# A new hand-out order for 2,900 operations, with one-element activations ahead of five table loads

## The chip, the cores and the metric

The kernel runs on one NeuronCore of a Trainium2 chip. Five engines each follow a queue of their own: TensorE (PE, matrix products), VectorE (DVE), ScalarE (ACT), GpSimd (POOL) and SyncE (SP), which issues all transfers of this kernel. Queues meet only through semaphores, and within a queue the order is fixed when the program is built. The metric is device time in microseconds; less is better. Three runs of the kernel before gave 535.62, 537.95 and 539.45 us, median 537.95.

## The reference

Two independent layers of width 576 over 2,048 positions, put side by side in the output. All data are float32.

```python
def _A_ref(u, log_A_real, A_imag, C_real, C_imag, log_dt, D_skip):
    dt = jnp.exp(log_dt)
    A = -jnp.exp(log_A_real) + 1j * A_imag
    C = (C_real + 1j * C_imag) * dt[:, None]
    P = jnp.exp((A * dt[:, None])[:, :, None] * pos[None, None, :])
    K = 2.0 * jnp.einsum("dn,dnl->dl", C, P).real
    y = irfft(rfft(u_t, 2L) * rfft(K, 2L))[:, :, :L]
    return y.transpose(0, 2, 1) + u * D_skip

def _B_ref(x, wqkv, w_phi, wo):            # 32 heads of 18
    q, k, v = split(x @ wqkv)
    pq, pk = q @ w_phi[h], k @ w_phi[h]
    phi = concat(softmax(p), softmax(-p))  # for q and for k
    kv, z = phi_k^T v, sum_s phi_k
    o = (phi_q kv) / (phi_q z + 1e-6)
    return o.reshape(B, S, D) @ wo
...
return jnp.concatenate([a, b], axis=-1)
```

Layer A is a long convolution: a kernel K of 2,048 taps for each of 576 channels is made from 128 complex modes and applied through a Fourier transform. Layer B is linear attention with a learned softmax feature map.

## The kernel before

**Layer B.** `fold` multiplies the feature map into the key and query weights (five blocks of heads; five products of up to 126 columns each, L448 by way of `mm`), and splits the result and the value and output weights (`whole`) into a high part `wh` and a remainder `wl`, so that a float32 product becomes three products of a faster type. `key_tile` takes one of 16 tiles of 128 positions: it loads x (`zo`), splits it (`x`, L542 and L463), multiplies it in three products of 378, 378 and 396 columns, makes the softmax features `e` and adds into one accumulator (`ps<-e,v`: 32 small products, one a head). `query_tile` does the same for queries, divides, and multiplies by the output weights. The first key product needs the first three folded blocks only; the second needs all five and a third of the value weights.

**Layer A.** `u_first` transforms the input (`ps<-kb,w`), in 16 steps. 18 pairs of channel groups (called group 0 to 17 here) make the convolution kernel: `phases` adds up integer phases on POOL into `cs` (a copy from `pi`, L899, and five doubling steps, L903; `cs` has two buffers, so a new pair waits until PE has read the old one), `waves` turns them into sines on ACT (L913, L920, L921), `group` multiplies them by exponentials on DVE (`cs`, `E`) and contracts them on PE (`ps<-E,cs`: 32 products for each half). `k_first`, `product` and `last` are the Fourier steps; they pass data through DRAM.

**What sets the order.** Each of these functions only records operations (`Plan.op`): an engine, or two of which either may do it, a function, and what it depends on. `Plan.run` then hands out all 2,900 in the sequence of the table `ORDER`. An entry `1143+2/2/8` is operation 1143, with 2 filler matmuls of zeros ahead of it (L227, they write a tile that the operation overwrites), and buffer slots 2 and 8 for the tiles that it opens; a `*` takes the second of its two engines. So the table sets the order in each engine's queue, the engine of the flexible operations (mostly copies out of PSUM, ACT or DVE, and element-wise operations on SBUF tiles, POOL or DVE), and which buffer is used again when. Semaphore waits follow from it.

**Table loads.** ScalarE holds one set of functions at a time. When the program is built, an ACT_TABLE_LOAD is put in front of an activation that needs another set. A wait for one semaphore is part of the activation itself, behind the load; where an activation waits for two, one wait stands as an instruction of its own in front of the load.

Of the kernel before, what the change touches and what calls it, by code (L numbers as in the profile page):

```python
# [170 lines left out]
class Plan:  # L171
# [58 lines left out]
    def run(self, order):  # L230
# [3 lines left out]
        for x in order:  # L234
            x, *slots = x.split("/")
            x, _, fill = x.partition("+")
            second, k = x.endswith("*"), int(x.rstrip("*"))
# [8 lines left out]
            self.emit(o, o[5][0] if second else o[0], int(fill or 0))
# [36 lines left out]
1197/12 239/1 1332 1333 1177/15 397 1289/10 383 1515 51/12 1339/1 1387 1388 1473/0 1334 271/0 1288 482 384/13 1307/14
1237/11 1335 1522 52* 1340 213/0 53 1474 1523/16 385 1290/3/7/1/6/1 1475 1166 1336 272/2 1294 1291 1252 1256/0 347/10
1255 386 1476 1342 1293 44 1525 270/0 388*/1 387 1477 55/6 274/2 1292 1337 278 389 1295 56/3 132/4 45 1349/13 1478
57/4 58/3 59 1533 60/5 275 1352 276/2 390 277 1338 1518 1479 1199/8 381/1 1198 391/12 1519/1 62 1697 1520 61 63 73
1348 1341 64*/4 65 1524 1343 158/18 279 214* 240/6 273/7 215 218/5 74 398 133* 392/5 280*/6 1344 393/0 66 67/17 1345
1346 289 1296 241* 54/1 394 1482 1480 1350 1200/6/0/3/4/8 1526 1207/12 242 223/1 217/1 1203 68/3 1202 1204 290 281*
1481 395 399 69/4 245/2 224 225/9 70* 1201 1527 1389/0 1390 1432/1 1433 348/11 1205 219/3 1239/8 221 1483 1434 1696
75* 1435 1528 1529 220 222 235 1436 1437 1488/0/10/7 1530 483 484 485 1531 1698 236* 282 1501/4/1/12 1486/7 1503/6  # L290
251/2 1484/5 1489 49/1 401/13 1546/1 246/3 71 1487 1217/1 226*/5 250 216/2 1491 283/17 1492 1206 1485 1504 1532 76 400
1438 227 1297/16 243/3 1490 1545 284/6 134 228 285/0 252/5 1277/6 244/0 263 229/4 1534 1699 1703 1535/17 1208/5 262
1502 1493 1353 1494 137/5 230/3 1536 104/4 286* 1537 455/17 1439 1440 1238* 248 231/4 1499/3 428/11 1538 287 143/1
1508 1354 247 1539 1495/2/13/0 154 232 1540 378/4 136/7 349* 253/5 1509 350 1700 1500 1496 249 135/5 138/4 254 1317/10
1507 1704 1505 237 255 1506 1510/0 1541 233 142 140 155 144/8 139 1240/3/6/4/5/6 256/8 351/6 291* 402/7 1511 1497 238
141 1244 320/3 429/10 1542 1543 1243 1242* 1241 1246 292 1267/7 1445/5/3/1 352/4 159/12 145*/6 1355 1441 1442 430*
257/3 293/8 258/2 431 353/3 1544 1219/11 146 1218 355/5 1705/1 356 1547/0 432/7 1245 1548 1549 1443/7 354/6 1550 1498
1551 359 1552 1715 358 147 1444 370 361/4 357/4 1707 1447/2 435/4 371 1449 1446 1448 360 1512 1513 362 105/9 1553 160*
1452 434/6 1450 363 1209 148/12 1451 1210/7/3/0/2/2 1453 1356 321/6 1212* 161 1454/5 450/5 364/18 452 1214 259 440/0
1213 1220/4/2/3/0/11 451 149/1 403 260 1211 185/12 1216 1223 1222* 1221 150/6 1224 1225 1458/7/1/3 1460/3 1462/2 365/5  # L300
1215 163/4 1459 1461 1464 1463 264 433/0 1554 151 1455 1465 1226 1468 1227/11 1257/18 366/4 439 404 156 1556 1466 1467
152 167/3 265 1555 441/2 1469/7 162/8 367 157 1706 166 1557 1558/2/10/11 437 368 1357 496/13 164/3 168/5 405/9 1470
# [125 lines left out]
def body(tc, nc, i, out, ctx):  # L428
    pl = Plan()
# [15 lines left out]
    B, op = pl.buf, pl.op  # L445
# [39 lines left out]
    hp = B("hp", [128, 1])  # L485
# [669 lines left out]
```

## Time and profile before

| what | value |
|---|---|
| median of 3 runs | 537.95 us (535.62 to 539.45) |
| the profiled execution | 534.13 us, its span 532.4 us |
| granted clock of TensorE | 0.997 |
| PE, DVE, ACT, POOL busy | 510.1, 453.9, 410.4, 331.8 us |
| moved by DMA | 115.97 MB, mean 218 GB/s |
| table loads of ScalarE | 42 |
| filler matmuls | 94 |

An engine is busy here while at least one of its instructions runs. A row of the timeline gives the start, the length, the engine, the line, the operation with what it writes and reads, how many instructions were merged, and in brackets the idle time of the engine ahead of them with what ended it. "issue" in that place is time in which the engine waited for nothing that the profile shows. The rows of the groups give the busy time, the mean duration of one in ns, and the idle time ahead. Times are from the start of the span.

### The profile page before, as it was taken

To read this page: it belongs to the slowest core of one execution; us is meant where nothing else is said; L and a number is where in the kernel's file an instruction comes from. 1 tells how busy PE (TensorE), PEld (TensorE's weight loads), DVE (VectorE), ACT (ScalarE), POOL (GpSimd) and SP (SyncE) were. 2 spreads that over 40 slices of the span, in tenths; PEclk is the share of its full clock that TensorE was granted. 3 is DMA by queue.
4 is the path that set the end of the run, shared out by engine and by line. 5 is a ranking of instruction groups with operands and counts; after the bars stand their busy time and mean duration, and the time that the engine had idled before them with its cause. 6 is when DMAs were issued, how large, how long until landed. Compare 5 with 4: busy or idle time off the path is not lost.

```text
span 532.4 us, 20329 instructions
## 1 busy us (share of the span) xinstructions
PE 510.1 (96%) x8502; PEld 421.4 (79%) x8502; DVE 453.9 (85%) x988; ACT 410.4 (77%) x727; POOL 331.8 (62%) x379
## 2 busy tenths in 40 slices
PE   8899999999999888999999999999999999999996
PEld 6799898999988676788886777866688886667975
DVE  3899998999998878999998999889987769887572
ACT  4799989999879968989999879789876455555442
POOL 1568899977988875894586478858373435323210
PEclk9999999999999989999999999999999999999999
DMA  8888994623426486375578755797575787996687
GB/s 261 290 331 244 278 318 139 211 80 143 143 79 196 119 285 204 81 234 142 158 225 298 247 180 173 235 287 244 167 245 170 249 247 234 282 337 220 216 306 214
DMA packets 80512, 115.97 MB, mean 218 GB/s; under 512 B 12452, under 2 KB 57636, under 8 KB 80420
## 3 DMA queue, kind: packets, MB, share of 16 engines
q1 hardware_dynamic: 80420, 114.67, 67.4%
q8 instruction: 67, 1.10, 0.8%
q14 instruction: 25, 0.20, 0.1%
HBM read 65.63 MB, written 49.01 MB: 215 GB/s over the span
## 4 chain that ended last, share of the span: by engine, by line
PE 68%; DVE 9%; ACT 8%; POOL 7%; DMA 4%; issue 3%; SPq 1%; POOLq 0%; ACTq 0%; DVEq 0%
PE ps L448 65%; POOL cs L903 3%; PE ps L700 2%; DVE ac L467 1%; POOL e L463 1%; DVE cs L948 1%; ACT e L593 1%; DMA e<-in_wkT_dram 1%; DMA mg<-gd 1%; ACT cs L920 1%; DMA ff<-in_ff_dram 1%; POOL wl L531 1%; ACT cs L913 1%; ACT cs L921 1%; DMA zo<-in_xT_dram 1%
## 5 line engine op out<-in xcount | busy, mean ns | idle before, releaser
L448 PE MATMUL ps<-wh,x 128*128 128x288 f32 (+2 forms) x1008 | 241.0, 319 | 2.7 <-ACT wh L514 1.9
L448 PEld LDWEIGHTS ps<-wh,x 128*128 128x128 f32 x1008 | 173.1, 188 | 14.9 <-ACT wh L514 2.2
L448 PE MATMUL ps<-wl,x 128*128 128x288 f32 (+2 forms) x560 | 175.2, 313 | 0.3 <-DVE wl L515 0.3
L448 PEld LDWEIGHTS ps<-wl,x 128*128 128x128 f32 x560 | 105.4, 188 | 1.5 <-DVE wl L515 0.6
L903 POOL TENSOR_TENSOR cs<-cs,pi 128x64 int32<-128x64 int32 (+4 forms) x90 | 92.2, 1025 | 6.1
L596 POOL TENSOR_TENSOR o<-e 128x576 f32<-128x576 f32 x32 | 42.6, 1333 | 33.7 <-ACT e L593 25.8
L463 POOL TENSOR_TENSOR E<-v,cs 128x512 f32<-128x512 f32 x30 | 38.1, 1290 | 26.4 <-ACT v L944 26.4
L467 DVE TENSOR_TENSOR ac<-us,ps 128x576 f32<-128x576 f32 x64 | 44.8, 744 | 7.2 <-PE ps L448 4.8
L448 PEld LDWEIGHTS ps<-E,cs 128*32 128x32 f32 x2304 | 34.2, 110 | 17.0 <-issue 8.9
L463 POOL TENSOR_TENSOR e<-e,small 128x576 f32<-128x576 f32 x31 | 36.8, 1186 | 14.6 <-DVE small L463 13.6
L448 PE MATMUL ps<-E,cs 128*32 128x64 f32 x2304 | 40.1, 220 | 5.9 <-issue 3.3
L948 DVE TENSOR_TENSOR cs<-ps,cs 128x1024 f32<-128x1024 f32 x36 | 43.6, 1212 | 2.0 <-ACT ps L937 1.7
L937 ACT ACTIVATE ps<-ps 128x512 f32<-128x512 f32 x72 | 41.7, 593 | 4.8 <-PE ps L448 4.2
L448 PE MATMUL ps<-sel,mg 128*128 128x512 f32 x108 | 42.8, 450 | 1.9 <-ACT zi L453 0.4
L593 ACT ACTIVATE e<-e 128x1152 f32<-128x1152 f32 x32 | 37.3, 1167 | 6.0 <-POOL e L463 5.8
L921 ACT ACTIVATE cs<-cs,hp 128x1024 f32<-128x1024 f32 x36 | 40.7, 1143 | 0.0
L453 ACT ACTIVATE zi<-ps 128x288 f32<-128x288 f32 x91 | 32.2, 414 | 8.9 <-PE ps L448 8.2
L463 POOL TENSOR_TENSOR e<-small,e 128x576 f32<-128x576 f32 x26 | 31.1, 1198 | 11.2 <-DVE e L467 4.0
L913 ACT ACTIVATE cs<-cs 128x2048 f32<-128x2048 int32 x18 | 34.6, 1922 | 4.2 <-POOL cs L903 4.2
L920 ACT ACTIVATE cs<-cs 128x1024 f32<-128x1024 int32 x36 | 36.8, 1053 | 0.3
L586 DVE TENSOR_REDUCE small<-ps 128x16 f32<-128x288 f32 (+2 forms) x64 | 28.2, 443 | 5.8 <-PE ps L448 4.0
L585 DVE TENSOR_REDUCE small<-ps 128x16 f32<-128x288 f32 (+2 forms) x64 | 28.4, 443 | 5.5 <-PE ps L448 5.1
(143 smaller groups left out, 1051.8 us busy)
## 6 DMA issues: line engine op xcount, KB each, us to landing
dram<-zi SPq DMA_DIRECT2D x32, 288.0 KB, 4.5
xd<-x SPq DMA_DIRECT2D x16, 576.0 KB, 4.6
x<-xd SPq DMA_DIRECT2D x16, 576.0 KB, 4.8
dram<-zi SPq DMA_DIRECT2D x16, 576.0 KB, 3.9
kb<-dram SPq DMA_DIRECT2D x32, 288.0 KB, 5.8
ub<-dram SPq DMA_DIRECT2D x32, 288.0 KB, 4.7
dram<-zo SPq DMA_DIRECT2D x32, 288.0 KB, 3.7
zi<-dram SPq DMA_DIRECT2D x16, 576.0 KB, 7.7
```

Of the source, the lines that this page charges most:

```text
L448: pe.matmul(o, l, r, start=start, stop=stop, skip_group_check=skip)
L453: op(("act", "dve"), (c_act(n), c_dve(n)), lambda e: act.activation(dst(), src(), AF.Copy) if e == "act" else dve.tensor_copy(dst(), src() ...
L463: op(eng, [c_dve(n[0]) if e == "dve" else c_pool(n[1]) for e in eng], lambda e: (dve if e == "dve" else pool).tensor_tensor(dst(), a(), b( ...
L467: op(eng, c_dve(n) if eng == "dve" else c_pool(n), lambda: e.tensor_tensor(dst(), a(), b(), op=alu), r=r, w=w, with_=with_, lock=eng == "p ...
L593: op("act", c_act(1152) + 40, lambda: act.activation(e.t, e.t, AF.Exp), r=[e], w=[e], table="exp")
L596: op("pool", c_pool(517), lambda: pool.tensor_tensor(pair.t, e.t[:, :, :, 0:9], e.t[:, :, :, 9:18], op=ALU.add), r=[e], w=[pair], lock=True)
L903: op("pool", c_add(4 * n * W), lambda n=n, j=j: pool.tensor_tensor(x()[:, :, :, n:2 * n], x()[:, :, :, 0:n], pi.t[:, j:j + 2, gs].bitcast( ...
L913: op(("act", "dve"), (c_act(n) + 45, c_dve(n)), lambda e: act.activation(cs.t[:, 0], x(), AF.Abs) if e == "act" else dve.scalar_tensor_ten ...
L920: op("act", c_act(64 * W) + 150, lambda at=at: act.activation(at(1), at(1).bitcast(I32), AF.Sin, scale=TURN), r=[cs], w=[sine], with_=[cs] ...
L921: op("act", c_act(64 * W) + 225, lambda at=at: act.activation(at(0), at(0), AF.Sin, scale=-TURN, bias=hp.t), r=[cs, hp, sine], w=[both], w ...
L937: op("act", c_act(512) + 12, lambda: act.activation(ps.t, ps.t, AF.Exp), r=[ps], w=[ps], table="exp")
L948: op("dve", c_dve(64 * W), lambda: dve.tensor_tensor(F(), both(M.t), F(), op=ALU.mult), r=[M, ready], w=[long], with_=[cs])
```

## The change

The table `ORDER` is replaced whole: the same 2,900 operations, with another sequence, other buffer slots (1,022 operations) and other engines. 266 operations change engine. Counted over the program, 109 copies and one absolute value or the like go from ACT to DVE and 51 copies the other way; 69 element-wise operations go from DVE to POOL and 37 from POOL to DVE. Filler matmuls go from 94 to 28, all 28 ahead of the first product of the program. The large-scale sequence of the stages on PE stays: key tiles 12, 8, 0, 6, 7 and so on, with groups 2, 1, 3, 0, 4, 8, 7, 5, 6 between them; what moves is mostly a few places.

A mark `!` is new: ahead of such an operation `early` issues an activation of one element a partition, from `hp` into the new tile `warm`, with the function set that the operation needs. The table load then stands in front of that activation, which has no wait of its own, and so ahead of all waits of the operation. Five operations carry it (147, 336, 1979, 2321, 2206). With them the program has 44 table loads.

```diff
@@ Plan.run
             x, *slots = x.split("/")
             x, _, fill = x.partition("+")
+            early, x = x.endswith("!"), x.rstrip("!")
             second, k = x.endswith("*"), int(x.rstrip("*"))
...
                     b.t = self.pools[b.tag].tile(b.shape, b.dt, name=b.name, tag=b.tag + slot)
+            if early:
+                self.early(o[6])
             self.emit(o, o[5][0] if second else o[0], int(fill or 0))
...
 ORDER = """
-0/0 2 1 3 261/0 4/1 153/2 234/3 374/4 33 396/5 12/1 72/6 288/7 19/8 1361 1360 40/2 46/0 375/3 1358 5/4 369/9 1359 26/5
...
+33 0/0 1 1358 1362 1360 1361 19/0 1366 1365 1367/1 1369 1368 4/2 1359 1370 2 1377 1371 20+28/0 1363/0 1372 1373 1364
...
-    tags({1: "zero ident w1 w3 hp dsk kvb wh wl sel dt th cre cim ax ay mn ld ldc",
+    tags({1: "warm zero ident w1 w3 hp dsk kvb wh wl sel dt th cre cim ax ay mn ld ldc",
...
-    hp = B("hp", [128, 1])
-    op("pool", 60, lambda: pool.memset(hp.t, math.pi / 2), w=[hp])
+    hp, warm = B("hp", [128, 1]), B("warm", [128, 1])
+    op("pool", 60, lambda: pool.memset(hp.t, math.pi / 2), w=[hp], with_=[warm])
+    pl.early = lambda table: act.activation(warm.t, hp.t, dict(exp=AF.Exp, sin=AF.Sin)[table])
```

The first place is SP's queue at the start of the program. `e`, `ub` and `kvb` with in_wkT are the five blocks of key weights, fT the feature map, zo the x tiles, in_wv the value weights, and cim, cre, dt and th small inputs of layer A. Before:

```order
L499 DMA fT<-in_wphi_dram 128x630
L490 DMA zo<-in_xT_dram 128x640
L503 DMA kvb<-in_wkT_dram 72x640
L503 DMA e<-in_wkT_dram 126x640
L503 DMA ub<-in_wkT_dram 126x640
L840 DMA cim<-in_cim_dram 128x96
L840 DMA cre<-in_cre_dram 128x96
L490 DMA zi<-in_wv_dram 128x960
L490 DMA cs<-in_wv_dram 128x960
L838 DMA dt<-in_ldt_dram 128x96
L503 DMA e<-in_wkT_dram 126x640
```

The same place now:

```order
L507 DMA kvb<-in_wkT_dram 72x640
L842 DMA dt<-in_ldt_dram 128x96
L844 DMA cre<-in_cre_dram 128x96
L844 DMA cim<-in_cim_dram 128x96
L507 DMA ub<-in_wkT_dram 126x640
L503 DMA fT<-in_wphi_dram 128x630
L844 DMA th<-in_aim_dram 128x96
L507 DMA e<-in_wkT_dram 126x640 x2
L494 DMA zo<-in_xT_dram 128x640
L507 DMA e<-in_wkT_dram 126x640
```

The key weights have moved ahead of the first x tile, and the value weights have gone behind all of them (five and nine rows further on).

The second place is POOL's queue where group 5's phases are made, while the last key tiles run. `v` is a value tile that is scaled, `e` a feature tile, `cs<-cs,pi` are the doubling steps. Before:

```order
L596 TENSOR_TENSOR o<-e 128x576
L463 TENSOR_TENSOR kb<-ub 128x288
L463 TENSOR_TENSOR small<-small 128x32
L899 COPY cs<-pi 128x64
L463 TENSOR_TENSOR v_2657<-v_2657,small 128x608
L903 TENSOR_TENSOR cs<-cs,pi 128x64
L463 TENSOR_TENSOR e<-e,small 128x32x18
L903 TENSOR_TENSOR cs<-cs,pi 128x64x2
L903 TENSOR_TENSOR cs<-cs,pi 128x64x4
```

The same place now:

```order
L600 TENSOR_TENSOR o<-e 128x576
L466 TENSOR_TENSOR kb<-ub 128x288 x2
L466 TENSOR_TENSOR v_1936<-v_1936,small 128x608
L903 COPY cs<-pi 128x64
L466 TENSOR_TENSOR e<-e,small 128x32x18
L907 TENSOR_TENSOR cs<-cs,pi 128x64
L907 TENSOR_TENSOR cs<-cs,pi 128x64x2
L907 TENSOR_TENSOR cs<-cs,pi 128x64x4
```

The scaling of v has moved from behind the copy to ahead of it; the scaling of e stays inside the chain of steps.

The third place is PE's queue where the two halves of group 7 are contracted, a little later. `fT,e` are products of the query fold, `sel,mg` those that make exponents, `ident,o` transposes. Before:

```order
L448 MATMUL ps<-sel,mg 128x512 x2
L448 MATMUL ps<-fT,e 128x72 x4
L670 MATMUL ps<-ident,o 36x128 x4
L448 MATMUL ps<-E,cs 32x64 x64
L448 MATMUL ps<-kb,w_210 64x288 x8
```

The same place now:

```order
L451 MATMUL ps<-sel,mg 128x512 x2
L451 MATMUL ps<-fT,e 128x126 x9
L451 MATMUL ps<-E,cs 32x64 x32
L451 MATMUL ps<-e,v_1558 19x36 x32
L451 MATMUL ps<-E,cs 32x64 x32
L674 MATMUL ps<-ident,o 36x128 x8
```

The two halves now have a key tile's 32 products between them, and the transposes follow instead of standing in front.

More of the change, by code (lines that the diff above doesn't have):

```diff
@@ L283 @@
[L283 to L302, printed above, removed]
@@ new lines @@
+2009/11 2534/3 880/5 2479 2478 881 2217 731/6 2481 2480 892/4 733/2 2536/5/2/4/3/15/10 2072 2538* 2539
+2543/6/7/1/0/3/8 2011* 2537* 2540 2547 2546 2545 2511/9 942 943/10 2513/0 882/2/4 883/12 884 2021/5/9/7 2022 2023/3
+2024/13 2073 732/0 734 2028 2482/2/3/7/1/1/17 2029 2019/5 2004/0 2224 885 2020 2486 2544 944/5 2491/7 886 945 1047
+894/6 2483 2025 2027* 2026* 2006/2 2005 2484 2010 2012* 2223 2225/11 2485 2226 2007 2014 2221/1 2227 2228 2074 2229
+2520/18 2013 2030/5 2548/7/3/1/4/13/10 2550 2235 2552 2230 2231 2447/5 899/0 893/2 2489/3 946* 2551 2232 2519/4 2233
@@ new lines @@
+2466 2134 2166 967/0 2164/3 2165/8 2148/6/1/4/2/7 2151 2150* 2142/7/3/0/5/9 2149* 2145* 2146* 2152 2143
+2499/2/1/4/6/5/6 2503 904/4 2500 905/0 2488 2557/7 2167* 2424/11 2501 2168* 2144 906 542/7 545/1 2171/2/3/8 2172* 2255
+2331/0 2256 2173 2332 2258 2154/1/6/5/3/0 2157 2502 2333 2158* 2155 2257 592/9 966/0 2174 968 544 2156* 546/2 2425/18
+2504/6/1/5/2/5/4 593/6 594 2259 2406/2 2506 2136/0/7/3/4/1 2507 907 2505* 2508* 2334 2137 2140* 2138* 2139*
+2426/2/5/6/1/3/9 2427* 2429* 2248 2260/7/13/5 2430* 908 2335 2336 2261 2428 2264/3 2265/11 913/4/18 914* 595 596 2465
@@ new lines @@
+2313* 2210 2330 2187 2207 576/2 2189 2211 578/6 2192 2421 747 2579/11 618 2196 2212/1 2213* 2194* 2823/4 1051/5
+2795/11 2214 2824/7/2/10 2825 2195 2826 2827 2796/6/4/16 2797* 2193* 2197/2 1050/4 2788/9 2737/5 1052 2798 748/3 668
+669 2799 2738/18 1053/0 2198* 670/9 2199 970/10 2314 1054 1055 2372 1057/1 575/0 2315 2215 2200 577 1056 2373 2829
+2828 2380/2/1/5/6/1 814/13 1058* 749/5 2384 671/0 2381* 750 751* 672 2374/0/4/7/3/2 2376 2378* 776/6 779/5 777/3
+2837/11 778 780/3 752 757/6/9 2800 2802/4 2830/12 2377 782 2382 2383 753/5/3 755/1/10 2385 2375 2379 1059 781 783
@@ L425 @@
+2844/12 2875 2876 2866/7/1/11 2867 2815 2859/5/0/0 1113/6 2878 2820 2868 2822 2869 1110/3 2821 2871 2860 846 2861 847
+1114/5 1111/0 2880/7/0/8 2881* 2882 2883 2884 2877 2852/2/1/5 2892 2853 2894/0/4/13 2895 2845/7/1/7 1115/2 1112
+1116/4/3 1117/12 696 2814 2854 848/6 2855 2896 2885 2856 2897 849/0 2857 2862 2864 2898 2846* 2847 1118 2870 1119 2863
+2848 850/16 2899 1120 1121/3 851* 2849 2850 1122/0 1124/11 1123* 852 1125
 """.split()
```

253 lines of the change are left out of this document (127 added, 126 removed).

## The prediction

> **What bounds the kernel now.** I read the page first, then the busy time by stage, then the waits, then stretches of the timeline and of the chain.
>
> ```profile
> span 532.4 us, 20329 instructions
> PE 510.1 (96%) x8502; PEld 421.4 (79%) x8502; DVE 453.9 (85%) x988; ACT 410.4 (77%) x727; POOL 331.8 (62%) x379
> ```
>
> ```profile
> 0.00:18.29 18.29, 14.01 (x112) 11.68 (x112) 8.38 (x22) 10.63 (x22) 3.44 (x15) 1.00 0.85 269
> ...
> 184.00:238.00 54.00, 47.09 (x871) 39.81 (x871) 47.63 (x106) 45.30 (x85) 40.86 (x46) 0.97 0.70 208
> 238.00:400.00 162.00, 158.73 (x3107) 123.10 (x3106) 148.47 (x328) 143.18 (x239) 107.49 (x115) 1.00 0.68 215
> 400.00:532.40 132.40, 126.69 (x1902) 99.31 (x1900) 93.95 (x212) 65.05 (x160) 40.70 (x41) 1.00 0.77 248
> ...
> 26.62:79.86 53.24, 52.86 (x686) 49.09 (x685) 51.60 (x102) 49.57 (x78) 43.64 (x48) 1.00 0.90 293
> ...
> 18.29:201.00 182.71, 176.60 (x2782) 158.55 (x2782) 168.72 (x349) 159.10 (x254) 151.84 (x177) 0.99 0.62 203
> ```
>
> The columns are the stretch, its length, the busy time of PE, weight loads, DVE, ACT and POOL, the granted clock, the DMA share and GB/s. TensorE is the main bound: it is idle for 22.3 us of 532.4, and no order of the same matmuls can take away more than that and what hides inside its busy time. But DVE stands right beside it in the first 200 us: 51.60 of 53.24 us busy in one stage, 168.72 of 182.71 up to 201. So a gain of PE there has to be matched by DVE. Two stretches let PE wait: the start, up to 18.29, and 184 to 238, where it is idle for 6.9 of 54 us.
>
> The sum is made against the profiled execution, 534.13 us, which has 1.7 us outside its span. The median of the runs shown is 537.95, 1.0072 times as long; I carry sums over by that ratio. One per cent (5.4 us) is about what a measurement of this kernel can tell from no change, since three runs of it spread over 0.7%.
>
> **The start.** PE's first real matmul waits for folded key weights, and these wait for a transfer.
>
> ```profile
> 5.57 0.54 SPq L503 DMA_DIRECT2D e<-in_wkT_dram  x1
> ...
> 8.71 0.34 SPq L503 DMA_DIRECT2D e<-in_wkT_dram  x1
> ```
>
> ```profile
> 7.51 1.13 PE L448 MATMUL ps<-fT,e 126*128 126x126 f32 x8 [0.31 <-DMA e<-in_wkT_dram]
> ...
> 11.03 1.93 PE L227 MATMUL ps<-ident,zero 128*128 128x126 bf16 x32
> 13.33 1.38 PE L448 MATMUL ps<-fT,e 126*128 126x126 f32 x10 [0.38 <-DMA e<-in_wkT_dram]
> ...
> 14.79 1.38 PE L448 MATMUL ps<-fT,e 126*128 126x126 f32 x10
> ...
> 18.29 0.44 PE L448 MATMUL ps<-wh,x 128*128 128x378 f32 x1 [1.91 <-ACT wh L514]
> ```
>
> ```profile
> 17.50 1.38 ACT L514 ACTIVATE wh<-ps 128x126 fp32r<-128x126 f32 x4
> 18.75 0.76 ACT L542 ACTIVATE x<-zo 128x640 fp32r<-128x640 f32 x1
> ```
>
> The block that PE waits for at 13.33 is the eleventh transfer of the queue. By the shapes in the order, 2.93 MB go up to and with it; at the stage's 269 GB/s that is 10.9 us, so it landed 2.4 us after what the rate alone gives. In the changed order the last of the first three blocks (the first key product needs only those) is the ninth transfer, and 1.67 MB go up to it, because the value weights (twice 0.49 MB) and x come later: 6.2 + 2.4 = 8.6 us. The x tile is the tenth, 2.00 MB: 7.4 + 2.4 = 9.8. Then ACT copies x (0.76), PSUM copies of the last block follow (four took 1.38), and DVE subtracts: 9.8 + 0.8 + 0.9 + 0.8 = 12.3 us for the first key product, 6.0 earlier than 18.29. The frequency parameters that the new order puts ahead on ACT and DVE have small inputs that lead the queue, and should be done before 8.6; if not, each microsecond of theirs is one less. Bounds: 4 to 7.5 us. The 66 filler matmuls that go (94 to 28) cost
>
> ```profile
> L227 PE MATMUL ps<-ident,zero 128*128 128x256 bf16 (+4 forms) x94 | 12.7, 291 | 1.7 <-DVE ident L481 1.7
> ```
>
> 12.7 us in all, but mostly in waits like 11.03 to 13.33, so I take 0. At most the 32 that stand behind the first key product are worth 32 x 0.29 = 9.3 us; if the clock falls without them to the 0.97 of the stage 184 to 238, that is 3% of such a stage, 1.6 us.
>
> **What DVE takes back.** The rows for work that changes engine:
>
> ```profile
> L463 DVE TENSOR_TENSOR e<-small,e 128x576 f32<-128x576 f32 x6 | 5.6, 932 | 0.1
> L463 DVE TENSOR_TENSOR x<-zo,x 128x512 fp32r<-128x512 f32 (+1 forms) x17 | 13.7, 813 | 4.0 <-ACT x L542 3.9
> L463 DVE TENSOR_TENSOR kb<-ub 128x288 f32<-128x288 f32 x23 | 13.4, 592 | 1.3 <-PE ps L448 1.3
> L453 DVE COPY zi<-ps 128x288 f32<-128x288 f32 x37 | 15.3, 443 | 4.0 <-PE ps L448 3.9
> L453 DVE COPY ks<-ps 128x128 f32<-128x128 f32 x7 | 2.0, 284 | 1.9 <-PE ps L448 1.9
> L453 DVE COPY v<-ps 128x396 f32<-128x396 f32 x2 | 1.1, 558 | 0.0
> ...
> L453 ACT ACTIVATE zi<-ps 128x288 f32<-128x288 f32 x91 | 32.2, 414 | 8.9 <-PE ps L448 8.2
> ```
>
> Over the whole kernel 58 PSUM copies net go from ACT to DVE (58 x about 0.41, 24 us less for ACT; x 0.44 for DVE, 25.7 more), and 32 additions or products net go from DVE to POOL (up to 32 x 0.59, 19 us, by the kb row), so DVE ends at least some 6 us fuller. What matters is when. Ahead of the second E,cs product of group 7 (202.39 in the trace) DVE must have done 389 instructions in the new order, 371 in the old: five e<-small,e more (4.7 us), four x<-zo,x (3.3), six ks copies (1.7), four v copies (2.2), three copies of 288 (1.3), single ones of v and e (about 1.6), less six kb (3.6). That is 11 us more.
>
> Before, 201.0 us was 9.9 idle ahead of 18.29 (18.29 - 8.38), 177.1 busy and 14.0 idle afterwards (182.71 - 168.72). Now the busy time is 188.1. Let the idle at the start shrink by half of the 6.0, to 6.9. Then the same point comes at 195.0 us plus DVE's later idle time. With none it is 195.0, which is also where PE's 6.0 us would put it; with the 3.1% idle of DVE's fullest stage (1 - 51.60/53.24) it is 188.1/0.969 + 6.9 = 201.0, and nothing is won; with the old 14.0 it is 209.0. I take the middle of the first two, since ACT and POOL, for which DVE waits, have some 3 us less to do each ahead of that point: 198.0, a gain of **3.0 us** of the start's 6.0.
>
> **184 to 238.**
>
> ```profile
> 187.31 0.87 PE L448 MATMUL ps<-E,cs 128*32 128x64 f32 x47
> 190.50 0.44 PE L448 MATMUL ps<-E,cs 128*32 128x64 f32 x17 [2.33 <-issue]
> ...
> 202.39 1.00 PE L448 MATMUL ps<-E,cs 128*32 128x64 f32 x57 [0.19 <-DVE E L467]
> 204.35 0.32 PE L448 MATMUL ps<-E,cs 128*32 128x64 f32 x7 [0.96 <-issue]
> ```
>
> ```profile
> 191.03 0.29 POOL L899 COPY cs<-pi 128x64 int32<-128x64 int32 x1 [2.23 <-PE ps L448]
> 191.24 1.22 POOL L463 TENSOR_TENSOR v<-v,small 128x608 f32<-128x608 f32 x1
> 192.42 0.41 POOL L903 TENSOR_TENSOR cs<-cs,pi 128x64 int32<-128x64 int32 x1
> ```
>
> POOL is idle for 2.23 us until PE frees cs, and then an unrelated v product of 1.22 us stands in the middle of the phase chain that DVE, ACT and PE wait for. In the new order it stands ahead of the copy, in that idle time: **1.2 us** off the chain, or 0 if another input of group 5 is late instead.
>
> The two waits on "issue" (2.33 and 0.96) come in the middle of one product, where no semaphore can hold PE, behind a dense run of small matmuls. Code comes in pieces:
>
> ```profile
> q8 instruction: 67, 1.10, 0.8%
> ...
> PE ps L448 <- issue: 3.9, 3, 2.3
> ```
>
> 1.10 MB in 67 is 16 KB each, and 20329 instructions make it a steady stream; I read these waits as code that was late. Counting pieces in the search could remove all 3.3 us. But the run e,v then kb,w then E,cs ahead of group 8 is still there with another key tile, and group 7 has become denser (E,cs, e,v, E,cs), so one more stall of 2.33 is as possible. Between -3.3 and +2.3 I take **0.8** off. The Trainium skill, page "Runtime: NRT & Kernel Launch", section "Instruction fetch mechanics", says that crossing a 16 KiB boundary is mostly hidden, since the next piece is fetched while the current one runs. By it this term is 0 and the total 0.8 us less of a gain; the trace speaks against "hidden" at these two places, and for it at nearly all others.
>
> **The table loads.** Loads go from 42 to 44; five of them now come with a one-element activation ahead of a wait.
>
> ```profile
> L920 ACT ACT_TABLE_LOAD x16 | 20.5, 1283 | 0.3
> ...
> 11.95 1.28 ACT L844 ACT_TABLE_LOAD   x1
> 13.24 0.28 ACT L844 ACTIVATE ax<-mn 128x96 f32<-128x96 f32 x1
> ```
>
> The largest group of loads has 0.3 us of idle ahead of sixteen: they already start as soon as ACT is free, with no wait to be moved past. Five activations of at most 0.28 us and two loads of 1.28 are 4.0 us of ACT, which is idle for 122 us and loses 24 us of copies. I take 0, between -1 and +4. The Trainium skill, page "ScalarE: Activation LUTs", section "What ACT_TABLE_LOAD costs", adds 1380 ns of drain to each load; here the next activation starts 10 ns behind it, so the trace shows none, and by the page the two loads would take 5.3 us of ACT instead of 2.6.
>
> **238 to the end.** PE idles 3.3 + 5.7 us there, and of the latter the last transfer takes
>
> ```profile
> out_dram<-ot SPq DMA_DIRECT2D x16, 288.0 KB, 4.6
> ```
>
> 4.6. The order of products is nearly the old one, and DVE and ACT have room for their exchanged copies, so I take **0.5** off the 4.4 that are left.
>
> The sum: -3.0 - 1.2 - 0.8 - 0.5 = -5.5, so 528.6 us for a profiled execution and 532.4 for the median.
>
> **The rivals.** First, DVE takes all of the start back, as in its fullest stage: 201.0 at group 7, and only 2.5 us of gain, 531.6, median 535.4. For it: that 96.9% was reached with all other engines full too. Second, slower: DVE's old 14.0 us of idle time are waits for others that the new order does not shorten. Then PE waits for DVE from the key tiles on, group 7 comes at 209.0, 8.0 later, and the total is +5.5: 539.6, median 543.5. It decides from a later idle time of DVE above 8.5 us up to 201 (6.0 plus the other 2.5). Against it: many of those waits are for PE itself, which comes earlier. Third, PE keeps all 6.0, both code stalls go (3.3), with 1.2 and 1.0 from the rest: -11.5, 522.6, median 526.4.
>
> **How the numbers follow.** The forecast has a chance of 0.44 (0.30 of it beyond 1%, as its centre lies on that line and its bounds reach further down), DVE's taking all back 0.22, slower 0.20, the large gain 0.14. So faster by over 1% is 0.44, within 1% 0.36, slower 0.20. The range takes in the centres of all four and leaves out the further half of the two at the ends, less than 2 in 10: 524 to 544. The forecast's own range is 528 to 537.
>
> **What would show it.** The first 128x378 product of PE at 11.5 to 14 us instead of 18.29; DVE busy for 96% or more between there and the second E,cs product of group 7, and that product at 196 to 201; the v product of POOL ahead of its copy, and no wait of over 1.2 us inside the phase chain; the "issue" waits of PE at 0 to 3 us in place of 3.9 in the waits; table loads with idle time near 0 ahead of them in both. The prediction is wrong if the first product is no earlier than 16, if DVE shows more than 8.5 us of idle time up to group 7, or if the difference arises behind 238.

## The result, and the profile after

The changed kernel takes 520.01 us (median of 4 runs, 519.47 to 521.60) where the kernel before takes 536.79 on the same chip; the ratio is 0.969 with a 95% interval of 0.964 to 0.974. The forecast was 532.4 in 524 to 544: the direction was right, the size was a third of the real one, and the time lies outside the range. The profiled execution took 519.47 us, its span 517.7, 14.7 less than before.

The head of the page, and the busy time by stage (stretch, length, PE, weight loads, DVE, ACT, POOL, clock, DMA share, GB/s). The stretches are those of before, moved to where the same amount of TensorE's work is done.

```profile
span 517.7 us, 20283 instructions
PE 491.1 (95%) x8436; PEld 411.7 (80%) x8436; DVE 453.7 (88%) x1014; ACT 396.1 (77%) x676; POOL 340.8 (66%) x411
```

```profile
0.00:19.21 19.21, 11.12 (x78) 9.44 (x78) 7.17 (x22) 7.34 (x17) 3.43 (x11) 1.00 0.78 210
19.21:201.00 181.79, 175.15 (x2891) 159.52 (x2895) 172.46 (x370) 155.49 (x244) 139.86 (x173) 0.99 0.62 198
184.00:234.60 50.60, 48.17 (x943) 39.30 (x943) 48.05 (x107) 47.62 (x80) 45.96 (x53) 1.00 0.67 194
234.60:388.30 153.70, 149.12 (x2999) 118.19 (x2998) 138.78 (x313) 143.12 (x241) 112.70 (x127) 1.00 0.71 221
388.30:517.70 129.40, 123.64 (x1993) 98.43 (x1992) 102.83 (x235) 56.81 (x126) 55.26 (x65) 1.00 0.87 275
```

TensorE's idle time did not fall: 532.4 - 510.1 = 22.3 before, 517.7 - 491.1 = 26.6 now (8.0 of it ahead of its first matmul, and 3.1 in one wait for a copy on DVE at 164 us). What fell is its busy time, by 19.0 us, for the same products. 66 of the filler matmuls account for 12.7 - 5.2 = 7.5 of it. With the fillers put to the idle time, that went from 35.0 to 31.8; so 3.2 of the 14.7 us are idle time and 11.5 are in the products themselves, as the groups show (busy time, mean ns of one, idle time ahead; the trace has two records for each of the float32 matmuls of ub,ff and kb,ff, and a record is called a product here). Before:

```profile
L448 PE MATMUL ps<-sel,mg 128*128 128x512 f32 x108 | 42.8, 450 | 1.9 <-ACT zi L453 0.4 <-DMA mg<-gd 0.3 <-DVE cs L948 0.3
L448 PE MATMUL ps<-ub,ff 64*32 64x288 f32 x512 | 21.1, 409 | 0.9 <-DMA ff<-in_ff_dram 0.9
L448 PE MATMUL ps<-kb,ff 32*32 32x288 f32 x512 | 17.4, 412 | 0.0
```

Now:

```profile
L451 PE MATMUL ps<-sel,mg 128*128 128x512 f32 x108 | 40.1, 440 | 1.6 <-DVE zi L456 1.2 <-DVE e L470 0.3
L451 PE MATMUL ps<-ub,ff 64*32 64x288 f32 x512 | 19.4, 408 | 0.2 <-ACT fT L456 0.2
L451 PE MATMUL ps<-kb,ff 32*32 32x288 f32 x512 | 12.8, 413 | 0.5 <-DVE us L456 0.2
```

The mean of one is the same, but the 512 kb,ff products together keep TensorE busy for 12.8 us instead of 17.4, with next to no idle time ahead of them in either. These small products run side by side: 32 of them at 0.41 us each take 0.78 us where they are densest. When one of them waits 0.2 us for its PSUM bank (PSUM holds TensorE's results; a bank is one of the eight slots of `ps`) while another (0.41 us) still runs, the wait counts as busy. One of the sixteen steps shows how. Product step 5 before, on PE, then on DVE:

```profile
309.99 1.13 PE L448 MATMUL ps<-ub,ff 64*32 64x288 f32 x25
311.05 0.51 PE L448 MATMUL ps<-sel,mg 128*128 128x512 f32 x1
311.40 0.63 PE L700 MATMUL ps<-ident,e 128*128 128x128 f32 x4
311.96 1.48 PE L448 MATMUL ps<-kb,ff 32*32 32x288 f32 x32
```

```profile
311.23 0.66 DVE L854 SCALAR_TENSOR_TENSOR ax<-cre,ax 128x96 f32<-128x96 f32 x1
311.81 0.45 DVE L467 TENSOR_TENSOR e<-ps,small 128x288 f32<-128x288 f32 x1
312.18 0.44 DVE L453 COPY us<-ps 128x288 f32<-128x288 f32 x1
```

The same step now, on PE and on ACT:

```profile
301.54 1.20 PE L451 MATMUL ps<-ub,ff 64*32 64x288 f32 x32
302.67 1.10 PE L451 MATMUL ps<-E,cs 128*32 128x64 f32 x64
303.70 0.78 PE L451 MATMUL ps<-kb,ff 32*32 32x288 f32 x32
```

```profile
302.42 1.42 ACT L456 ACTIVATE us<-ps 128x288 f32<-128x288 f32 x4 [1.42 <-PE ps L451]
```

Before, the kb,ff products overwrite banks of the ub,ff products, and one of those banks is read until 312.62 by a copy that stood on DVE behind two other steps: 1.48 us for 32 products. Now a whole E,cs group stands between the two, ACT has made the four copies meanwhile, and the same 32 products take 0.78.

Where the 14.7 us come from: the two traces are lined up by work done, each product counting with the typical time to the next product's start of its kind (the 20th percentile before, 459 us in all). The times now and the gains are worked out so and stand in no view; done over by operations of the table, they differ by up to 1.9 us.

| work done, at the time before | time now | gained in the stretch |
|---|---|---|
| 201.0 | 200.0 | 1.0 |
| 238.0 | 235.1 | 1.9 |
| 320.0 | 313.7 | 3.4 |
| 400.0 | 388.6 | 5.1 |
| 532.4 (end) | 517.7 | 3.3 |

What a product takes beyond its typical time sums to 67.2 us before and 46.0 now. I call it "late bank" where the last reader of a PSUM bank that the product overwrites ended less than 0.4 us ahead of the product's start, or later: 23.5 us before, 10.3 now. This counts all that such a product takes too long, and a wait ahead of its first bank goes to the product before it. By operations of the table the same rule gives 23.5 and 15.0, so the sign is firm and the size is not. Waits for other inputs fall from 9.0 to 3.1. The start's share falls by 6.2, but TensorE also begins 6.3 us later, so that is no gain.

### The profile page after: what moved, and what is told of

It reads as the page before. It is cut to its first block, busy times and chain, and to the rows that moved or that the text cites. A ratio compares the mean times of both kernels' runs of the same rounds, so it can differ in the third digit from the quotient of the medians.

```text
span 517.7 us, 20283 instructions
## 1 busy us (share of the span) xinstructions
PE 491.1 (95%) x8436; PEld 411.7 (80%) x8436; DVE 453.7 (88%) x1014; ACT 396.1 (77%) x676; POOL 340.8 (66%) x411
## 4 chain that ended last, share of the span: by engine, by line
PE 67%; DVE 13%; ACT 10%; issue 4%; DMA 2%; SPq 1%; POOL 1%; DVEq 0%; ACTq 0%; POOLq 0%
PE ps L451 63%; PE ps L704 2%; ACT ps L941 1%; PE ps L734 1%; ACT cs L925 1%; ACT cs L924 1%; DVE e L466 1%; ACT L941 1%; PE ps L227 1%; POOL cs L907 1%; DMA ub<-in_u_dram 1%; DMA xd<-x 1%; ACT e L597 1%; DVE ac L470 1%; DVE E L470 1%
## 5 line engine op out<-in xcount | busy, mean ns | idle before, releaser
L451 PEld LDWEIGHTS ps<-wh,x 128*128 128x128 f32 x1008 | 173.7, 189 | 13.6 <-issue 5.3
L466 POOL TENSOR_TENSOR E<-v,cs 128x512 f32<-128x512 f32 x34 | 43.3, 1292 | 8.9 <-ACT v L948 8.8
L952 DVE TENSOR_TENSOR cs<-ps,cs 128x1024 f32<-128x1024 f32 x36 | 43.5, 1213 | 1.8 <-ACT ps L941 1.7
L466 POOL TENSOR_TENSOR e<-e,small 128x576 f32<-128x576 f32 x29 | 34.4, 1188 | 11.0 <-DVE small L466 10.5
L451 PE MATMUL ps<-sel,mg 128*128 128x512 f32 x108 | 40.1, 440 | 1.6 <-DVE zi L456 1.2
L889 POOL TENSOR_TENSOR pi<-pi 128x192 int32<-128x192 int32 (+1 forms) x42 | 20.6, 506 | 21.2 <-DVE pi L885 20.9
L466 POOL TENSOR_TENSOR e<-small,e 128x576 f32<-128x576 f32 x23 | 26.9, 1170 | 11.5 <-DVE small L466 6.2
L456 ACT ACTIVATE zi<-ps 128x288 f32<-128x288 f32 x76 | 26.9, 416 | 9.8 <-PE ps L451 9.7
L917 ACT ACTIVATE cs<-cs 128x2048 f32<-128x2048 int32 x17 | 32.6, 1917 | 0.8 <-POOL cs L907 0.7
L466 POOL TENSOR_TENSOR ac<-ac 128x288 f32<-128x288 f32 x31 | 24.1, 803 | 12.9 <-DVE ac L470 9.5
```

Source lines behind the costliest of these rows:

```text
L451: pe.matmul(o, l, r, start=start, stop=stop, skip_group_check=skip)
L456: op(("act", "dve"), (c_act(n), c_dve(n)), lambda e: act.activation(dst(), src(), AF.Copy) if e == "act" else dve.tensor_copy(dst(), src() ...
L466: op(eng, [c_dve(n[0]) if e == "dve" else c_pool(n[1]) for e in eng], lambda e: (dve if e == "dve" else pool).tensor_tensor(dst(), a(), b( ...
L917: op(("act", "dve"), (c_act(n) + 45, c_dve(n)), lambda e: act.activation(cs.t[:, 0], x(), AF.Abs) if e == "act" else dve.scalar_tensor_ten ...
L952: op("dve", c_dve(64 * W), lambda: dve.tensor_tensor(F(), both(M.t), F(), op=ALU.mult), r=[M, ready], w=[long], with_=[cs])
```

## The experiments

Each run is compared with runs of before on the same chip (median there 536.5 to 537.0). The working theories came up one after the other.

### Half tables: is the gain in the late part?

x1 takes the table of before up to 201 us and the new sequence behind it, x2 the reverse; x9 and x10 do the same at 238 us, where the two tables have handed out nearly the same operations.

```diff
 x1:  ... 534 1804 488/10
-1792/5 1803 1009/3 510 580/5 ...
+536 527/2 528 529 530 ...
 x9:  ... 1762 1958 648/2/7
-2039/0 698/3 2044 2043/1 2066/0 ...
+1189* 698/4 1765 1766/3 649/13 ...
```

> The table of before up to the point where TensorE stood at 201 us, and from there the remaining operations in the sequence of the new table (58 buffer slots had to be chosen anew at the seam). Theory A: the gain arises behind 201 us, where the matmuls of the Fourier stages wait for PSUM banks that copies on DVE and ACT free too late; then this kernel has nearly all of it, 12 to 14 us less than before, ratio 0.973 to 0.978. Theory B: the new early part sets up the later gain (buffers and transfers that lie further ahead); then at most 5 us, ratio 0.99 or above.

> The new table up to the same point, then the remaining operations in the sequence of before. Theory A: 0 to 3 us less than before, ratio 0.994 to 1.00, with DVE-freed PSUM banks late behind 201 as before. Theory B: 8 us or more less, ratio 0.985 or below.

> Old table up to the point where TensorE stood at 238 us, new sequence for the rest. The seam is chosen where the two tables have handed out nearly the same operations (10 differ), so that only 6 PSUM banks and rows are chosen anew instead of over 50. Theory A (the late sequence gains by itself, and x1 lost its time at the seam): 9 to 13 us less than before, ratio 0.976 to 0.984. Theory B (the two parts only work together): ratio 0.995 or above.

> The counterpart: new table up to 238, old sequence for the rest. Theory A: 1 to 5 us less than before, ratio 0.991 to 0.998. Theory B: slower than before, ratio 1.005 or above.

| run | median us | ratio (interval) |
|---|---|---|
| x1, late part new, from 201 | 541.19 | 1.007 (1.004 to 1.011) |
| x2, early part new, to 201 | 554.51 | 1.031 (1.027 to 1.036) |
| x9, late part new, from 238 | 535.36 | 1.001 (0.997 to 1.005) |
| x10, early part new, to 238 | 536.51 | 1.001 (0.997 to 1.005) |

Theory A falls: no half keeps the gain. x1 and x9 lie where theory B put them (0.99 or above, 0.995 or above), but x2 and x10 do not: the new early part does not gain 8 us, and at 238 it is not slower than before. The halves cut at 201 are slower than either whole. Lined up with the new kernel behind 303 us, where both do the same operations in the same order, x9's late part runs at the same pace, but falls back in a few single steps of 0.7 to 3.4 us. TensorE's waits hold the largest of them (engine, line, waited for: us, times, longest):

```profile
PE ps L451 <- issue: 7.9, 7, 2.3
```

That is 7.9 us against 2.7 in the new kernel; 2.8 of it lie in the old part, as in before, and 5.1 behind the seam, where the new kernel has 1.7. x9's late part has the same products, but 89 instructions of TensorE's more ahead of them; x13 below takes this up.

### Sequence or engines?

x3 gives the old sequence the new engines, x4 the new sequence the old engines; only the `*` marks change (266 of them).

```diff
-1767 ... 1864 ... 1858* ... 1862*
+1767* ... 1864* ... 1858 ... 1862
```

> The sequence and slots of before, but every flexible operation on the engine that the new table gives it. Theory A1 (the sequence carries the gain): within 4 us of before on either side, ratio 0.993 to 1.007. Theory A2 (the exchanged copies carry it, since a copy on the less loaded engine frees its bank earlier): 6 to 12 us less, ratio 0.978 to 0.989.

> The new sequence and slots, with every flexible operation on the engine of before. Theory A1: 2 to 5 us slower than the new kernel, ratio to before 0.973 to 0.978, since the sequence was made for other engines. Theory A2: most of the gain gone, ratio 0.985 or above.

x3: 580.75 us, ratio 1.081 (1.076 to 1.085). x4: 568.85, ratio 1.061 (1.057 to 1.066). Both theories fail: neither the sequence nor the choice of engines carries the gain, and either with the other's partner costs 32 to 44 us against before. The number of TensorE's instructions is that of the parent table in both (to within one), and the waits on issue are 2.5 and 1.6 us, so this is not the place of the code. Late banks come to 40.4 us in x3 and 38.0 in x4. The head of x3's page shows the form that it takes:

```profile
span 578.5 us, 20320 instructions
PE 532.8 (92%) x8502; PEld 432.5 (75%) x8502; DVE 479.0 (83%) x1014; ACT 396.0 (68%) x669; POOL 346.2 (60%) x411
```

TensorE is busy for 22.7 us longer with the same 8,502 matmuls, and idle for 23 us longer. Within a queue the order is fixed, so a copy on another engine at the same place in the table stands behind something else, and its bank comes free late; I take this for the reason, no run takes it apart.

### Is it the amount of DVE's work?

```diff
-dve.tensor_tensor(F(), both(M.t), F(), op=ALU.mult)
+dve.tensor_tensor(F()[:, 0], M.t, F()[:, 0], op=ALU.mult)
```

> Before, with the product of cosines and sines by the first exponentials on DVE (cs<-ps,cs, 36 times 1.21 us) cut to its first half of 512 columns, so the second half of the modes keeps values that are not multiplied: some 0.6 us less of DVE and of its PSUM bank in each of 36. Theory C: the gain of the new table is time in which TensorE waited for banks that DVE still read, inside what counts as busy; before has these waits, so it falls by 6 to 12 us (ratio 0.978 to 0.989), and its busy TensorE falls with it. Theory D (the gain is not in late DVE reads): 0 to 3 us (0.994 to 1.00).

> The new kernel with the same cut. Theory C: its banks are free in time already, so 1 to 4 us less than the new kernel (ratio to before 0.961 to 0.967), and the distance to the cut kernel of before shrinks from 17 to under 11 us. Theory D: both lose the same, distance 15 us or more.

x5: 536.24 us, ratio 1.001 (0.997 to 1.005). x6: 520.85, ratio 0.974 (0.967 to 0.981). Theory C falls as I had put it: with the product down from 43.6 to 24.4 us in x5 and from 43.5 to 24.3 in x6 (DVE is busy for 11.3 and 17.1 us less in all), neither kernel is faster, and the distance is still 15.4 us, as theory D had it. Late banks stay too: 24.4 us in x5, 8.8 in x6. So they do not come from how long this step takes; that leaves its place in the queue and what it waits for.

### Only the bank numbers

```diff
-2006/2 2030/5 2548/7/3/1/4/13/10 893/2
+2006/4 2030/7 2548/6/3/1/5/13/10 893/5
```

> The new kernel with the same sequence and engines; only the numbers of the PSUM banks change (437 tiles): each product takes, among the banks that are free in the table, those that by the trace of the new kernel come free at most 0.2 us after it wants to start. By that trace the late banks add up to 13.7 us instead of 3.5. Theory C2 (late banks cost TensorE their time, as busy and not as idle): 6 to 12 us slower than the new kernel, ratio to before 0.980 to 0.991, with kb,ff, ac,ff, sel,mg busy for longer and idle time nearly unchanged. Rival (products overlap such waits with others): 0 to 3 us slower, 0.969 to 0.975.

x11: 525.76 us, ratio 0.982 (0.977 to 0.988). That is theory C2 by its ratio; the 5.8 us against the new kernel are just under its range in us. Sequence, engines and work are those of the new kernel. Late banks rise from 10.3 to 21.8 us. The page and two views:

```profile
span 524.8 us, 20275 instructions
PE 496.7 (95%) x8436; PEld 412.6 (79%) x8436; DVE 454.2 (87%) x1014; ACT 396.4 (76%) x676; POOL 340.2 (65%) x411
```

```profile
L451 PE MATMUL ps<-kb,ff 32*32 32x288 f32 x512 | 14.0, 413 | 1.0 <-issue 0.9
```

```profile
PE ps L451 <- issue: 5.3, 6, 1.5
```

Of the 7.1 us that the span grows, 5.6 are busy time of TensorE and 1.5 idle. Some 2.6 us of it may be waits for code (5.3 against 2.7, at places that moved by up to 7 instructions), so late banks account for 4.5 to 7.1. This shows that late banks cost time and look mostly like work. It also shows that the count above overstates them: 11.5 us more of late banks made the span 4.5 to 7.1 longer. At that rate the 8.5 to 13.2 us that the new table takes off are worth some 4 to 8 of the 14.7 (an estimate). ac,ff, which I had named too, did not grow.

### Small parts: late fillers, early table loads

```diff
 x7:
-1300+13/7/2/6/1/3  2514+7/0/4/5/6/2/5
+1300/7/2/6/1/3  2514/0/4/5/6/2/5
 x8:
-147! 336! 1979! 2321!/9 2206!/6
+147 336 1979 2321/9 2206/6
```

> Before without the 32 filler matmuls that stand behind the first key product (at 309, 322 and other places behind 200 us). If they only fill waits: ratio 0.997 to 1.001. If they stand on the path with their 3.8 us busy time: 0.991 to 0.995. If the clock needs them: above 1.003.

> The new kernel without the five one-element activations, so the table loads stand directly ahead of the activation that needs them. As forecast (loads start without a wait anyway): 0 to 1 us on either side of the new kernel, ratio to before 0.967 to 0.971. Rival (a load behind a wait costs its 1.28 us each on the path): 2 to 6 us slower than the new kernel, 0.973 to 0.980.

x7: 537.16 us, ratio 1.001 (0.997 to 1.005): no gain from the fillers alone. The reading isn't clean, since it also moves the code behind them by 26 to 61 instructions. x8: 519.23, ratio 0.970 (0.964 to 0.976), as the new kernel. The five marks are worth nothing that can be measured; TensorE's code lies at the same places in both.

### The start

```diff
-33 0/0 1 1358 1362 1360 1361 19/0 1366 1365 1367/1 1369 1368 4/2 1359 1370 2 1377 1371 20+28/0
+33 0/0 2 1 1358 1362 1360 1361 19/0 1366 1365 1367/1 1369 1368 4/2 1359 1370 1377 1371 20+42/0
```

> The new kernel with the zeroing of the filler tile put first on DVE (in the new table it stands behind seven parameter steps, at 7.8 us, and all of TensorE waits for it) and 42 fillers instead of 28, so that they run from 1.7 to about 9.5. The first 128x378 product comes at 14.5 to 16.5 us instead of 19.2. Theory S1 (the start passes through to the end): 2.5 to 4.5 us less than the new kernel, ratio to before 0.960 to 0.965. Theory S2 (DVE takes it back, as I forecast for half of it): 0 to 1.5 us, 0.966 to 0.970. Theory S3 (the weights land later than the fillers last, and the granted clock falls): 1 us slower or more.

In the new kernel every product waits for the tile of zeros, which DVE writes late: behind four parameter steps, which wait for three on ACT and these for small transfers. PE and DVE of the new kernel:

```profile
7.98 5.17 PE L227 MATMUL ps<-ident,zero 128*128 128x256 bf16 x28 [7.98 <-DVE zero L486]
12.99 1.28 PE L451 MATMUL ps<-fT,ub 126*128 126x126 f32 x10
14.10 1.28 PE L451 MATMUL ps<-fT,e 126*128 126x126 f32 x10
15.22 1.24 PE L451 MATMUL ps<-fT,kvb 72*128 72x72 f32 x10
16.29 2.92 PE L451 MATMUL ps<-fT,e 126*128 126x126 f32 x20
19.21 0.44 PE L451 MATMUL ps<-wh,x 128*128 128x378 f32 x1
```

```profile
7.81 0.11 DVE L486 MEMSET zero<- 128x64 uint32 x1
```

x12 starts its first 128x378 product at 15.05 us, but takes 521.08 us, ratio 0.974 (0.967 to 0.981). It is 3.9 us ahead of the new kernel at 201 us, 2.6 at 238, 1.9 at 400 and behind it at the end (span 519.0). By its time that is S3 (1 us slower or more) or, within the noise, S2, but neither cause is there: the granted clock is full up to 517 us, and no other engine took it back. Two waits on issue of 1.12 and 1.97 us between 189 and 202 us, where the new kernel has one of 0.43, account for the first loss. Its 14 more fillers move TensorE's code by 28 instructions.

### Where the code lies

x13 is x9 with 44 fillers fewer, so that the late part's code lies as in the new kernel. x14 has the early zeros and 28 longer fillers: the code lies as in the new kernel. x15 and x18 differ from x14 by more and shorter fillers only, so that the code moves by 128 and 64 instructions; x16 and x17 do the same to before.

```diff
 x13: -7+32/6 1300+13/7/2/6/1/3 1143+2/2/8     +7/6 1300+3/7/2/6/1/3 1143/2/8
 x14: -self.data.t[...][:, 0:n]                +self.data.t[...][:, None, 0:180].to_broadcast([rows, 2, 180])
 x15: -20+28/0, n of 360                       +20+92/0, n of 96
 x18: -20+28/0, n of 360                       +20+60/0, n of 168
 x16: -13+26/0, n of 256                       +13+90/0, n of 74
 x17: -13+26/0, n of 256                       +13+58/0, n of 115
```

> The kernel of x9 (old table up to 238 us, new behind) with 44 of the filler matmuls ahead of the seam left out (the 32 ahead of a fold step, 12 ahead of group 5), so that TensorE's instructions behind the seam stand at the same place in their 16 KB pieces as in the new kernel (in x9 they stand 89 further on; one piece holds 256). Theory F (in x9 the late sequence gains, but TensorE waits for code at new places, 7.9 us on issue against 2.7): the issue waits fall to 3 to 5 us and the time to 525 to 531, ratio 0.980 to 0.990. Rival G (the late sequence gains only behind its own early part): ratio 0.996 or above, whatever the issue waits.

> The new kernel with the zeroing of the filler tile first on DVE, and the 28 fillers of 360 columns instead of 256, so that they last as long as 42 did and TensorE's code stands exactly where it stands in the new kernel (in x12 it was moved by 28 instructions). First 128x378 product at 14.5 to 16 us. Theory F: the 4 us of the start, which x12 kept up to 190 us and lost to 3.1 us of issue waits there and to further ones, now pass through in part: 516 to 518.5 us, ratio 0.960 to 0.966. Rival S2 (another engine takes it back): 519 to 521.5 us, 0.967 to 0.972.

> The same start with 92 fillers of 96 columns: TensorE's code behind them is moved by 128 instructions, half a piece, and nothing else changes. Theory F: other issue waits, 5 us or more in all, and 3 to 8 us slower than x14. Rival: within 1.5 us of x14.

> Before with 90 fillers of 74 columns in place of the first 26 of 256: they last as long, but TensorE's code behind them is moved by 128 instructions, half a 16 KB piece. Theory P (the old sequence lies at an average place, and most of the gain of the new table is where its code lies): within 5 us of before on either side, ratio 0.991 to 1.009, so that with both codes moved by half a piece the two sequences differ by less than 6 us (x15: 536.3). Theory Q (the new sequence gains by itself): 8 to 16 us slower than before, ratio 1.015 to 1.030.

> The same with 58 fillers of 115 columns, a move by 64 instructions. Theory P: ratio 0.991 to 1.009. Theory Q: ratio 1.010 to 1.025.

> The kernel of x14 with its code moved by 64 instructions (60 fillers of 168 columns). By x14, x12 and x15 (moves of 0, 28 and 128: 516.6, 521.1, 536.3 us) 522 to 532 us, ratio 0.972 to 0.991, issue waits of TensorE of 5 to 12 us. If only some places are bad: within 3 us of x14, 0.96 to 0.966.

| run | code moved by | median us | ratio (interval) | issue waits of PE | late banks |
|---|---|---|---|---|---|
| before | 0 | 536.79 | 1 | 3.9 | 23.5 |
| x17 | 64 | 546.17 | 1.012 (1.007 to 1.018) | 5.7 | 24.6 |
| x16 | 128 | 547.57 | 1.020 (1.017 to 1.024) | 10.6 | 22.3 |
| new kernel | 0 | 520.01 | 0.969 (0.964 to 0.974) | 2.7 | 10.3 |
| x14, zeros first | 0 | 516.63 | 0.960 (0.955 to 0.965) | 1.9 | 11.7 |
| x12, zeros first | 28 | 521.08 | 0.974 (0.967 to 0.981) | 5.1 | 13.2 |
| x18, zeros first | 64 | 525.73 | 0.978 (0.974 to 0.983) | 10.1 | 11.7 |
| x15, zeros first | 128 | 536.28 | 0.999 (0.995 to 1.002) | 13.6 | 14.7 |
| x13, half table | 0 behind the seam | 532.11 | 0.990 (0.985 to 0.995) | 5.9 | 19.0 |

The waits and late banks are those of the profiled execution, which for x16 and x17 is their fastest (541.39 and 540.14). x14 against x15 is the plainest: same sequence, engines, banks and work behind the fillers, nearly 20 us apart, where theory F had 3 to 8. In the profiled executions they are 15.9 apart, of which 11.7 are waits on issue. For x18 against x14 it is 8.2 of 8.9, for x16 against before 6.7 of 7.3, but for x17 only 1.8 of 6.0, so the table does not explain x17. TensorE in x15, where two halves of a group's contraction follow each other, and the same place in x14:

```profile
70.79 1.56 PE L451 MATMUL ps<-E,cs 128*32 128x64 f32 x97
76.28 0.87 PE L451 MATMUL ps<-E,cs 128*32 128x64 f32 x23 [3.94 <-issue]
77.08 0.80 PE L451 MATMUL ps<-sel,mg 128*128 128x512 f32 x1
77.67 0.53 PE L451 MATMUL ps<-wh,x 128*128 128x396 f32 x1
```

```profile
72.29 1.99 PE L451 MATMUL ps<-E,cs 128*32 128x64 f32 x128
74.60 0.50 PE L451 MATMUL ps<-sel,mg 128*128 128x512 f32 x1 [0.32 <-DVE e L470]
74.94 0.34 PE L451 MATMUL ps<-wh,x 128*128 128x396 f32 x1
```

128 products with their weight loads are 256 instructions, one piece of 16 KB, used up in 2 us. In x15 TensorE stops in the middle of the run; the trace's records of the instruction queue have a piece fetched from 74.00 on, for 0.94 us, and TensorE goes on at 76.28. The next products then take 0.53 us instead of 0.34: the granted clock is 0.50 from 76.0 on, for 3.4 us.

The traces settle what these waits are. All 20 together have 102 waits of TensorE on issue. Counting TensorE's own instructions (matmuls, weight loads and its semaphore instructions), 101 of them come 192 or 193 behind a multiple of 256, whatever product stands there, and nearly all 2.2 to 2.8 us after the fetch of a piece began. So they are waits for code at the ends of pieces. A move by a whole piece, which by this should change little, was not run. The Trainium skill, page "Runtime: NRT & Kernel Launch", section "Instruction fetch mechanics", calls crossing a 16 KiB boundary mostly hidden; by it x14, x15 and x18 would take the same time, and the measurement (516.6, 536.3 and 525.7 us) decides against it where small products follow each other densely.

At equal moves the new sequence is ahead by 16.8 us (0: new kernel against before), 20.4 (64: x18 against x17) and 11.3 (128: x15 against x16); the latter two also have the early zeros, worth some 3 us by the medians of x14 and the new kernel. Theory P falls and Q holds: moving the code costs the old sequence 10 us as well, so the sequence itself is worth about 8 to 17 us at the moves tried, and of these both tables as they stand have the best. x13 shows the same for the graft: lined up with the new kernel's places it has 1.1 us of waits on issue behind the seam where x9 has 5.1 (its other 4.8 lie in the old part, whose code has moved), and it gains 1% that x9 did not show, at the upper end of theory F and 1.1 us beyond it. Behind 303 us it loses 3.1 us to the new kernel, x9 7.3. About half of its late banks lie in its old part; what it loses around the seam stays open.

x14 is the fastest of all kernels here: 516.63 us (515.16 to 517.85), 3.4 below the new kernel by the medians, though the two intervals of the ratio just touch. Its TensorE starts like this:

```profile
1.38 6.87 PE L227 MATMUL ps<-ident,zero 128*128 128x360 bf16 x28 [1.38 <-DVE ident L484]
8.09 1.28 PE L451 MATMUL ps<-fT,ub 126*128 126x126 f32 x10
...
16.05 0.45 PE L451 MATMUL ps<-wh,x 128*128 128x378 f32 x1
```

## Why the prediction was wrong

**238 to the end** is the step that failed: "so I take 0.5 off the 4.4 that are left", where 3.4 + 5.1 + 3.3 = 11.8 us came. The prediction had set the limit at TensorE's idle time "and what hides inside its busy time", and then priced the hidden part at nothing. In that part of the profile the kb,ff row had 17.4 us for 16 steps, 1.09 each, while the densest of the sixteen take 0.77. That comparison was there to be made before, and it would have shown some 5 us in this one row. What the runs show in its place: 11.5 us less busy time in the same products, over the whole kernel. x11 shows that such time is real and that late banks make it; their part is 4 to 8 us by the estimate above. Waits for other inputs fell by 5.9 us by the same count as the late banks, which no run takes apart, so how the rest divides stays open.

**The start**, -6.0 and half of it taken back, gained 1.0 by 201 us. The first 128x378 product came at 19.21, 0.9 later than before, past the 16 us that I had named as proof of error. I had followed the transfers and the ACT and DVE steps, and not the tile of zeros that all of TensorE waits for, behind the parameter steps, nor TensorE's own queue: from 7.98 to 19.21 the 28 fillers (5.17 us) and fifty fold products follow one another without a gap, and all of these stand ahead of the first key product. So the fillers, taken at 0, are in part on the path there: an estimate is up to 3 us, since x14 has its second block of key weights by 10.84 and the new kernel takes it at 14.10. x12 and x14 have the zeros first and start at 15.05 and 16.05, so even then 12.3 was too early: with 1.48 us of waiting for key weights in x14, fold products run up to the first key product.

That half of the start is taken back failed too. Of x14's 3.2 us at the start, 2.1 were left at 201 us and 2.4 at 400 (1.6 in the span), but the 1.1 were lost in one place, between 164 and 168 us of the new kernel's time, and not to DVE. There TensorE waits about 3 us for a copy in all three of these kernels. Behind it the granted clock is 0.50 for 6.8 us in x14, for 3.4 in the new kernel and not at all in x12, which gains 0.8 there. Nine microseconds around that wait, in the columns above, in x14, in the new kernel and in x12:

```profile
159.00:168.00 9.00, 7.08 (x94) 5.88 (x95) 7.48 (x17) 5.27 (x9) 6.10 (x10) 0.62 0.50 161
162.00:171.00 9.00, 6.88 (x101) 5.92 (x105) 8.32 (x18) 5.63 (x10) 7.17 (x10) 0.81 0.63 200
159.00:168.00 9.00, 7.11 (x163) 5.57 (x166) 8.87 (x17) 6.22 (x12) 7.70 (x10) 1.00 0.60 182
```

**What DVE takes back.** DVE should have been 188.1 us busy by 201; it was 7.17 + 172.46 = 179.6, 2.5 more than before instead of 11. The count of its instructions was right (390 against 373 ahead of that point, where I had 389 and 371), but two rows were priced by a wrong form. Of the four x<-zo,x more, three are 64x128, at 0.29 us and not 0.81; and of the v copies there are five more of 180 columns, at 0.33 us, and one less of 396, at 0.56. Besides, steps that both kernels have took less: the 15 small<-small 0.26 us instead of 0.44, the x<-zo,x of 128x512 0.70 instead of 0.96; why is not shown. Its later idle time was 9.3 us, beyond the 8.5 from which the slower rival was to decide, and still the second E,cs product of group 7 came at 200.32 instead of 202.39, since the 8.5 went with a busy time of 188.1. So DVE's idle time by itself decides nothing; x5 and x6 say the same with its busy time 11.3 and 17.1 us shorter.

**POOL** in group 5's phases went as forecast: from the start of the copy to the end of the last step they take 6.5 us instead of 7.6. From 201 to 238 1.9 us were gained; 1.0 of that is the wait for code at 204.35, which is gone. POOL in the new kernel:

```profile
189.57 1.33 POOL L466 TENSOR_TENSOR v<-v,small 128x608 f32<-128x608 f32 x1
190.85 0.29 POOL L903 COPY cs<-pi 128x64 int32<-128x64 int32 x1
```

**Code.** Issue waits fell from 3.9 to 2.7. That is close to the 0.8 that I took off, but by luck: the two waits of 2.33 and 0.96 went down to 0.64 and 0.43 in that stretch, and a new one of 1.40 came at 285 us.

```profile
PE ps L451 <- issue: 2.7, 4, 1.4
```

The reading of these waits as late code was right; my upper end of +2.3 for what another place can cost was far too small: x15 has 13.6 us of them.

**Table loads** at 0 were right (x8), and the longest groups still have no idle time ahead. **Fillers** at 0 agree with x7 for the 32 late ones, as far as that run can tell; not at the start, as said.

```profile
L924 ACT ACT_TABLE_LOAD x18 | 23.1, 1283 | 0.3
```

**The rivals.** The large gain (-11.5) was nearest, but for other reasons: all of the start and both code stalls; the start did not come, and the code gave 1.2. Between them the cases had no mechanism by which a product waits while it counts as busy, and so the range ended too high.

## What to carry to other kernels

Where many small products run side by side, compare a group's busy time for one step with its densest step: the difference is waiting, here in good part for PSUM banks, and a better order can win it though the idle time shows nothing. Sequence, engines and buffer numbers of an order table belong together; half of it can cost more than the whole wins. Compare forms and not only rows when a step is priced: a row's mean mixes them. Before an edit to such a kernel is judged, keep the instruction count ahead of dense runs, or try the edit at several places of the code: here a move of 128 instructions was worth as much as the whole new table.

## What was not expected of the hardware

A run of 128 small products (256 instructions) takes 2 us, and a wait for code inside one was up to 3.94 us, with the next products slower by half (0.53 against 0.34 us). The place of the code alone moved the new sequence from 516.6 to 536.3 us and the old one from 536.8 to 547.6. And a step on DVE that took 19.2 us less in all, on an engine that is 85% busy, changed nothing (536.24 against 536.79 us); DVE's busy time fell by 11.3 us only.
